# A windowed attention with a soft mixture of experts: the same steps in another hand-written order

## The chip, the cores and the metric

The program runs on one core of one Trainium2 chip. A core has five engines that run side by side, each through its own instructions in program order: TensorE (matrix products, PE in the profile; its loads of stationary operands are shown apart as PEld), VectorE (DVE), ScalarE (ACT), GpSimd (POOL) and SyncE (SP), which here issues nearly all DMA transfers. An instruction waits on semaphores until what it needs has been signalled; whatever stands behind it on the same engine waits with it. The metric is the device time of one execution in microseconds (us). Three runs of the kernel before took 214.01 to 214.91 us, the median is 214.57 us.

## The reference

The input is q, k and v of 4 batches, 8 heads, 768 positions and head width 64, and the weights of a soft mixture of 8 experts.

- Attention: scores q·k/8 plus a bias that falls with the distance (slope by head), over the 96 keys up to the position itself and 8 global keys; softmax over the keys; times v. The result, x, has 3072 tokens of width 512.
- Mixture: logits = x·phi (32 slots); softmax over the tokens gives the dispatch weights, and 32 slot inputs are weighted sums of tokens. Each expert runs its 4 slots through relu(s·w1)·w2 (512 to 1024 to 512). Softmax over the slots gives the weights with which each token mixes the 32 slot outputs.

```
scores = scale * q @ k.T + bias ; a = softmax(where(keep, scores, -1e9)) ; x = a @ v
logits = x @ phi ; d = softmax(logits, axis=0) ; slots = d.T @ x
out    = softmax(logits, axis=1) @ concat_e( relu(slots[e] @ w1[e]) @ w2[e] )
```

## The kernel before

**Units.** The attention is cut into 16 units u = 0 to 15 of one batch and two heads (a pair of heads, i = 0 and 1). The keys of a unit are cut into seven blocks of 120, each with the 8 global keys, and the queries that see a block are the 216 from its start. The steps of one unit, with their engine and the line that the profile gives for them:

- `load_qk(u)`, `load_v(u)` (SP, L389 and L392): the two transfers of the unit, into two buffers each (`raw`, `vt`) that take turns.
- `scores(u, k)`, k = 0, 1, 2 (PE, L521): products of keys and queries into one of two PSUM tiles `sc`, which also take turns.
- `biased(u, k)` (DVE, L530): adds the bias table, writes to `tb` and keeps a running maximum. The PSUM tile is free again behind it.
- `max_t(u)` (PE, L537) and `max_r(u)` (DVE, L542): maximum over the partitions.
- `exponential(u, i)` (ACT, L546), then `w_hi(u, i)` (ACT, L549; `w_hi_dve` on DVE, L552): the weights of head i, and their high part in 16 bits into `ph`.
- `w_lo(u, i, part)` (POOL, L556; `w_lo_dve` the same on DVE, also L556): the low part, in three pieces for each head.
- `v_hi(u)` (POOL, L489), `v_hi_act(u)` (ACT, L492) and `v_lo(u)` (DVE, L499): high and low part of V.
- `values(u, i)` (PE, L573): 39 products of the weights of head i with V into bank i of the one PSUM tile `x`; the text calls `values(u, 0)` the first product with V of a unit and `values(u, 1)` the second.
- `ev_sums(u)` (DVE, L586), `ev_recs(u)` (L592), `ev_mul(u, 0)` and `ev_mul(u, 1)` (L598): row sums, their reciprocals, and the scaling of X of each head out of `x` into `xn`; the scaling also keeps a maximum (`xmax`).
- `tr(u, k)` (PE, L610) and `tr_copy(u, k)` (ACT, L615; `tr_copy_dve` on DVE, L619): X transposed, in two parts.
- `logits` (PE, L640) every second unit; behind each batch the dispatch: `logits_all`, `strip_max`, `strip_exp`, `by_token` (PE, L696), `dispatch` (PE, L719), `dispatch_sum` (DVE, L730).

**The one tile `x`.** Both heads of a unit are written into one PSUM tile, and the waits that the compiled program gets go by that tile, not by its banks: a first product of unit u+1 waits for every scaling of unit u that stands ahead of it in the program, and a scaling of unit u that stands behind it waits for that product. (In the compiled program, `ev_mul(2, 1)`, which stands behind `values(3, 0)`, carries a wait for TensorE; where it stands ahead it carries none.)

```
565    x = xx[:, i]
573    nc.tensor.matmul(out=x[:, (D + 1) * t:(D + 1) * t + d], lhsT=w[:, c:c + P], rhs=vv[:, j, i, 0:d], ...
598    nc.vector.tensor_tensor_reduce(
599        out=xnb[(u // 2) % 3][:, :, c:c + D], in0=xv[:, i, :, 0:D], ...
819    for name, u, *args in ORDER:
820        steps[name](u, *args)
```

**What sets the order.** Nothing schedules at run time. `ORDER` (L51) is a list of 603 steps written out; the loop at L819 issues them in that order, and so each engine's program is the part of the list that falls to it.

**Weights.** w1 and w2 are 32 pieces of 1 MB each. Ten go into buffers of their own during the attention (`piece`, L372), some into holes of the attention's buffers (`extra`), and thirteen into those buffers when their last use is over (`free`). The rest follow when the first layer of the experts has used up its own buffers.

**The end.** Behind the last unit: the last dispatch (`last_dispatch`, L746), the first layer of the experts (`hidden`, PE, L106), transposes, the second layer (`project`, PE, L136), and the mixing of slot outputs with the output transfers (`combine`, PE, L196; copies L199 and L201).

Of the kernel before, what the change touches and what calls it, by code (L numbers as in the profile page):

```python
# [275 lines left out]
def tile_attention_moe(ctx: ExitStack, tc: tile.TileContext, qk, v, phi, w1, w2, nn, out):  # L276
# [64 lines left out]
    held = []  # L341
    for name, i, *_ in ORDER:
        if name == "free":
# [95 lines left out]
    def late_constants():  # L439
        nc.gpsimd.tensor_tensor(out=i4, in0=ident[:, 0:32], in1=ident[:, 32:64], op=ALU.add)  # L440
        nc.gpsimd.tensor_tensor(out=i4, in0=i4, in1=ident[:, 64:96], op=ALU.add)
        nc.gpsimd.tensor_tensor(out=i4, in0=i4, in1=ident[:, 96:128], op=ALU.add)
        nc.gpsimd.memset(sl, 0.0)
# [374 lines left out]
    late_constants()  # L818
    for name, u, *args in ORDER:  # L819
        steps[name](u, *args)  # L820
# [295 lines left out]
```

## Time and profile before

| | |
|---|---|
| median of three runs | 214.57 us (214.01 to 214.91) |
| the profiled execution | 215.71 us |
| its span, first to last instruction | 213.7 us |
| share of the span busy: PE, DVE, ACT, POOL | 84%, 69%, 59%, 45% |
| the 16 DMA engines | 61.38 MB, mean 287 GB/s |
| mean granted clock of TensorE | 0.971 of full speed |

The profiled execution took 1.14 us more than the median, and 2.0 us of it lie outside the span. The page of the profile gives the engines' busy time, the span in 40 slices, and the costliest groups of instructions. A view of waits adds up who stood idle for whom ("A <- B: us in total, times, longest"). A timeline lists instructions with their start, their duration and, in brackets, the idle time of the engine just before and what ended it. A table of windows gives the busy time of each engine in a stretch of time, with the granted clock and the DMA engines' share. The chain of waits is followed back from the last instruction.

### The profile page before, as it was taken

The numbers are of one execution on the slowest core, as the hardware profiler recorded it, in microseconds if no ns is written. First come the engines' busy times: TensorE is split into PE (matmuls) and PEld (weight loads), VectorE is DVE, ScalarE is ACT, GpSimd is POOL, SyncE is SP. The second block draws the span as 40 slices with busy tenths as digits, with TensorE's granted clock in tenths as the row PEclk, the third lists the DMA queues.
The fourth block names the chain that finished last, engine by engine and source line by source line (L and its number), as shares of the span: only waits on it lengthen the run. The fifth ranks groups of instructions, "written<-read, shape, count | busy, mean of one in ns | idle before, by whom it ended". The sixth has DMA issues, their size and how long they took to land.

```text
span 213.7 us, 6390 instructions
## 1 busy us (share of the span) xinstructions
PE 180.1 (84%) x2633; PEld 129.7 (61%) x2633; DVE 148.0 (69%) x382; ACT 125.9 (59%) x158; POOL 96.8 (45%) x122
## 2 busy tenths in 40 slices
PE   8999779699999899979897699588799999798400
PEld 2455679587878678667766588465353276475400
DVE  4869878479888597987977868877667745153600
ACT  2108768579998698897795879861303462041500
POOL 7113977567987688896584858430000000000000
PEclk9999999889999999999999999999999999999965
DMA  5946696748999999965538169959999999849892
GB/s 150 412 157 228 175 356 239 267 179 243 374 398 371 418 336 356 375 223 191 176 125 315 44 229 306 405 178 407 395 405 349 408 404 386 308 154 340 288 337 85
DMA packets 20630, 61.38 MB, mean 287 GB/s; under 512 B 1904, under 2 KB 9328, under 8 KB 18928
## 3 DMA queue, kind: packets, MB, share of 16 engines
q1 hardware_dynamic: 20448, 60.89, 77.4%
q8 instruction: 22, 0.36, 0.7%
q14 instruction: 16, 0.13, 0.2%
q10 hardware_dynamic: 144, 0.00, 0.0%
HBM read 54.59 MB, written 6.29 MB: 285 GB/s over the span
## 4 chain that ended last, share of the span: by engine, by line
PE 53%; DVE 17%; DMA 13%; ACT 7%; issue 4%; DVEq 0%; ACTq 0%; SPq 0%
PE sc L521 12%; PE x L573 12%; DMA raw<-in_qk_dram 8%; PE hp L106 6%; DVE tb L530 6%; DMA raw<-in_w_dram 5%; PE x L510 4%; PE x L136 3%; DVE xn L598 3%; ACT tb L546 3%; PE wp L424 2%; ACT ph L549 2%; PE m L640 2%; PE cp L196 2%; PE m L610 2%
## 5 line engine op out<-in xcount | busy, mean ns | idle before, releaser
L556 POOL TENSOR_TENSOR ph<-tb,ph 128x432 f16<-128x432 f32 x89 | 90.2, 1043 | 40.5 <-ACT ph L549 33.8
L573 PE MATMUL x<-v,ph 128*128 128x65 f16 (+1 forms) x1248 | 43.8, 194 | 10.2 <-DVE xmax L598 9.9
L573 PEld LDWEIGHTS <-ph 128*128 128x128 f16 x1248 | 41.7, 98 | 15.4 <-issue 14.2
L521 PE MATMUL sc<-raw 64*128 64x216 f32 (+2 forms) x448 | 48.3, 349 | 3.2 <-DVE mx L530 1.7
L546 ACT ACTIVATE tb<-tb,nb 128x1296 f32<-128x1296 f32 x32 | 44.0, 1375 | 9.3 <-DVE nb L542 9.3
L549 ACT CAST ph<-tb 128x1296 f16<-128x1296 f32 x31 | 39.4, 1271 | 15.5 <-PE x L573 13.5
L521 PEld LDWEIGHTS sc<-raw 64*128 64x128 f32 x448 | 38.2, 193 | 11.5 <-issue 4.8
L598 DVE CUSTOM_DVE_ANT_1 xn<-x,rc 120x448 f32<-120x448 f32 x32 | 19.6, 622 | 6.5 <-PE x L573 5.8
L530 DVE CUSTOM_DVE_ANT_1 tb<-sc,tt,mx 128x864 f32<-128x864 f32 x16 | 17.8, 1115 | 3.8 <-PE sc L521 3.4
L499 DVE SCALAR_TENSOR_TENSOR v<-vt,v 128x896 f16<-128x896 f32 x16 | 20.3, 1266 | 0.0
L492 ACT ACTIVATE v<-vt 128x896 f16<-128x896 f32 x14 | 13.2, 946 | 7.1 <-DMA vt<-in_v_dram 7.1
L610 PE MATMUL m<-ident,xn 120*128 120x120 f32 x105 | 16.4, 276 | 0.7 <-DVE al L657 0.4
L610 PEld LDWEIGHTS m<-ident,xn 120*128 120x128 f32 x105 | 10.8, 141 | 3.7 <-issue 1.6
L136 PE MATMUL x<-wp,vt 128*32 128x256 f32 x112 | 10.9, 381 | 1.1 <-DVE flag L856 1.1
L530 DVE CUSTOM_DVE_ANT_1 tb<-sc,tt 128x864 f32<-128x864 f32 x8 | 8.4, 1054 | 4.3 <-PE sc L521 4.0
L106 PE MATMUL hp<-wp,sl 128*32 128x512 f32 x80 | 10.5, 593 | 0.0
L530 DVE CUSTOM_DVE_ANT_1 tb<-sc,xta,mx 128x864 f32<-128x864 f32 x8 | 8.9, 1116 | 1.6 <-PE sc L521 1.3
L530 DVE CUSTOM_DVE_ANT_1 tb<-sc,xtt,mx 128x864 f32<-128x864 f32 x8 | 8.9, 1113 | 0.9 <-PE sc L521 0.6
L510 PE MATMUL x<-const-bfloat16-1.0 128*1 128x512 bf16 x37 | 8.7, 379 | 0.0
L199 ACT COPY tb<-cp 128x512 f32<-128x512 f32 x4 | 2.1, 590 | 10.9 <-PE cp L196 10.9
L199 ACT COPY ph<-cp 128x512 f32<-128x512 f32 x8 | 4.3, 604 | 6.4 <-PE cp L196 5.8
L136 PEld LDWEIGHTS x<-wp,vt 128*32 128x32 f32 x112 | 5.5, 110 | 3.8 <-DVE flag L856 1.2
(197 smaller groups left out, 261.0 us busy)
## 6 DMA issues: line engine op xcount, KB each, us to landing
raw<-in_qk_dram SPq DMA_DIRECT2D x15, 832.0 KB, 5.9
wp<-in_w_dram SPq DMA_DIRECT2D x10, 1024.0 KB, 8.5
vt<-in_v_dram SPq DMA_DIRECT2D x16, 448.0 KB, 5.8
wp<-in_w_dram SPq DMA_DIRECT2D x10, 512.0 KB, 7.5
out_dram<-ph SPq DMA_DIRECT2D x8, 512.0 KB, 6.9
tb<-in_w_dram SPq DMA_DIRECT2D x3, 1024.0 KB, 7.9
wp<-in_w_dram SPq DMA_DIRECT2D x8, 256.0 KB, 6.0
raw<-in_w_dram SPq DMA_DIRECT2D x8, 256.0 KB, 5.6
```

Source lines behind the costliest of these rows:

```text
L106: nc.tensor.matmul(out=hp[n][32 * s:32 * s + 32, :], lhsT=slv(a, c, s), rhs=w1(e, c // 2)[:, (c % 2) * DF + 512 * n:(c % 2) * DF + 512 * n ...
L136: nc.tensor.matmul(out=o[32 * s:32 * s + 32, 0:w], lhsT=ht[:, c, 32 * s:32 * s + 32], rhs=w2(4 * a + s, half)[:, c0 + c * w:c0 + c * w + w ...
L499: nc.vector.scalar_tensor_tensor(out=vlo[k].rearrange("p j i d -> p (j i) d"), in0=vraw[k].rearrange("p j i d -> p (j i) d"), scalar=V_SC, ...
L510: nc.tensor.matmul(out=xx[0:1, 0], lhsT=busy_in[:, 0:1], rhs=busy_in, start=True, stop=True)
L521: nc.tensor.matmul(out=z[:, i, at:at + n], lhsT=r_[r, KCOL[j]:KCOL[j] + KR], rhs=r_[r, KW + KB * j:KW + KB * j + n], start=True, stop=True)
L530: nc.vector.tensor_tensor_reduce(out=tb(u)[:, :, BW * k:BW * k + BW], in0=sc[(3 * u + k) % 2][:, :, 0:BW], in1=table.unit(u % NP, k), scal ...
L546: nc.scalar.activation(out=t, in_=t, func=AF.Exp, bias=nbs[u], scale=T_SC)
L549: nc.scalar.copy(out=blocks(phi_[i])[:, :, 0:QW], in_=tb(u)[:, i].rearrange("p (s c) -> p s c", c=QW))
L556: (engine or nc.gpsimd).tensor_tensor(out=blocks(plo_[i])[:, c, 0:QW], in0=tb(u)[:, i].rearrange("p (s c) -> p s c", c=QW)[:, c], in1=bloc ...
L573: nc.tensor.matmul(out=x[:, (D + 1) * t:(D + 1) * t + d], lhsT=w[:, c:c + P], rhs=vv[:, j, i, 0:d], start=(z == 0), stop=(z == len(ops) - ...
L598: nc.vector.tensor_tensor_reduce(out=xnb[(u // 2) % 3][:, :, c:c + D], in0=xv[:, i, :, 0:D], in1=rcs.pop((u, i)).unsqueeze(2).to_broadcast ...
L610: nc.tensor.transpose(out=m[:, at:at + KB], in_=xnb[(u // 2) % 3][:, t, P * (p % 2):P * (p % 2) + P], identity=ident[0:KB, 0:KB])
```

## The change

Only the list `ORDER` differs. It has the same 603 entries in number and the same work, issued in another order; the functions are untouched. Counted over the list:

- Low parts on VectorE (`w_lo_dve`): ten instead of seven (`w_lo` on GpSimd 86 instead of 89).
- Copies of the transposed X on VectorE (`tr_copy_dve`): six instead of eight (`tr_copy` on ScalarE 26 instead of 24).
- The one `w_hi_dve` (unit 15) becomes a `w_hi` on ScalarE.
- V's high part is made on GpSimd for units 11 and 15 instead of 0 and 8.
- Both scalings of a unit stand ahead of the next unit's first product for units 0 to 13. Before, the second one stood behind it for units 2, 5, 6, 12, 13 and 14; unit 14 is still so.
- The transfers: `load_v(1)` is the first one instead of the sixth; the ten pieces and most of the extras are spread differently among the loads of the units, the first piece later and the last ones later.

The list is one line of code in the file; here places of it are set apart in lines.

```diff
-ORDER = [('load_qk0', 0), ('load_phis', 0), ('load_qk', 0), ('keys', 0), ('scores', 0, 0),
+ORDER = [('load_v', 1), ('load_qk0', 0), ('load_phis', 0), ('load_qk', 0), ('keys', 0), ('table_even', 0),
...
-('ev_recs', 1), ('load_v', 3), ('max_r', 3), ('load_qk', 6), ('ev_mul', 1, 0), ('exponential', 3, 0),
-('v_hi_act', 3), ('biased', 4, 1), ('biased', 4, 2), ('ev_mul', 1, 1), ('values', 2, 0), ('scores', 5, 0),
+('ev_recs', 1), ('biased', 4, 1), ('ev_mul', 1, 1), ('load_qk', 5), ('tr', 0, 0), ('w_lo', 2, 0, 2),
+('ev_mul', 1, 0), ('piece', 2), ('scores', 5, 0), ('biased', 4, 2), ('w_lo', 2, 0, 1), ('w_lo', 2, 0, 0), ('values', 2, 0),
...
-('ev_recs', 11), ('scores', 14, 2), ('ev_mul', 11, 0), ('tr', 10, 0), ('logits_half', 9), ('biased', 14, 1), ('exponential', 13, 0),
-('v_hi_act', 13), ('biased', 14, 2), ('ev_mul', 11, 1), ('v_lo', 13), ('values', 12, 0),
+('ev_recs', 11), ('w_lo', 12, 0, 0), ('max_t', 13), ('load_qk', 15), ('ev_mul', 11, 1), ('max_r', 13), ('ev_mul', 11, 0),
+('biased', 14, 0), ('scores', 14, 1), ('logits', 9), ('w_lo', 12, 1, 2), ('biased', 14, 1), ('load_v', 14), ('values', 12, 0),
...
```

**TensorE, around the first product of unit 2.** `raw_93` and `raw_94` hold the q and k of even and odd units, `sc_167` and `sc_168` are the two score tiles, `ph_98` the weights of head 0, `ph_99` those of head 1. The loads of weights for L573 and most of its rows are left out. Before:

```order
L521 MATMUL sc_168<-raw_93 128x216 x4
L521 MATMUL sc_167<-raw_93 128x216 x2
L521 MATMUL sc_167<-raw_93 128x168 x2
L521 MATMUL sc_167<-raw_93 128x48 x2
L610 MATMUL m<-ident,xn_106 128x120 x4
...
L573 MATMUL x<-v_100,ph_98 128x65
...
L521 MATMUL sc_168<-raw_94 128x216 x4
L521 MATMUL sc_167<-raw_94 128x216 x4
L537 MATMUL m<-ident,mx 128x128
```

and with the change:

```order
L521 MATMUL sc_168<-raw_93 128x216 x4
L521 MATMUL sc_167<-raw_93 128x216 x2
L521 MATMUL sc_167<-raw_93 128x168 x2
L521 MATMUL sc_167<-raw_93 128x48 x2
L610 MATMUL m<-ident,xn_106 128x120 x4
L521 MATMUL sc_168<-raw_94 128x216 x4
...
L573 MATMUL x<-v_100,ph_98 128x65
...
L521 MATMUL sc_167<-raw_94 128x216 x4
L537 MATMUL m<-ident,mx 128x128
```

The first score step of unit 5 (`sc_168<-raw_94`) has moved ahead of the first product of unit 2.

**VectorE, the scalings of unit 11.** `tb_97` is the table buffer of unit 14, `xn_105` where the scaled X goes; a row with one output of one element reads out the running maximum of the row ahead. Before:

```order
L586 TENSOR_TENSOR rsall<-x,eps 120x14
L542 ISA m,nb<-m,shift 128x128
L542 ISA nb 128x1
L592 RECIPROCAL rc<-rsall 120x14
L598 ISA xn_105,xmax<-x,rc 120x7x64
L598 ISA xmax 120x1
L530 ISA tb_97,mx<-sc_168,xta,mx 128x2x432
L530 ISA mx 128x1
L530 ISA tb_97,mx<-sc_167,xta,mx 128x2x432
L530 ISA mx 128x1
L598 ISA xn_105,xmax<-x,rc 120x7x64
```

and with the change:

```order
L586 TENSOR_TENSOR rsall<-x,eps 120x14
L592 RECIPROCAL rc<-rsall 120x14
L598 ISA xn_105,xmax<-x,rc 120x7x64
L598 ISA xmax 120x1
L542 ISA m,nb<-m,shift 128x128
L542 ISA nb 128x1
L598 ISA xn_105,xmax<-x,rc 120x7x64
L598 ISA xmax 120x1
L530 ISA tb_97,mx<-sc_167,xta 128x2x432
L530 ISA mx 128x1
L530 ISA tb_97,mx<-sc_168,xta,mx 128x2x432
```

The two bias steps that stood between the scalings now come behind both; only the reduction of a maximum is between them.

**VectorE, between the scalings of unit 13 and the sums of unit 14.** `ph_99<-tb_97` are low parts of unit 14, `ph_98<-tb_95` and `ph_99<-tb_95` those of unit 15, L619 the copies, L552 the high part of unit 15, L499 V's low part. Before:

```order
L598 ISA xn_106,xmax<-x,rc 120x7x64
L598 ISA xmax 120x1
L556 TENSOR_TENSOR ph_99<-tb_97,ph_99 128x2x216
L619 COPY xta<-m 128x480
L619 COPY xta<-m 128x288
L556 TENSOR_TENSOR ph_99<-tb_97,ph_99 128x2x216
L552 CAST ph_98<-tb_95 128x6x216
L499 SCALAR_TENSOR_TENSOR v_100<-vt,v_100 128x896
L556 TENSOR_TENSOR ph_98<-tb_95,ph_98 128x2x216 x3
L586 TENSOR_TENSOR rsall<-x,eps 120x14
```

and with the change:

```order
L598 ISA xmax 120x1
L542 ISA m,nb<-m,shift 128x128
L542 ISA nb 128x1
L556 TENSOR_TENSOR ph_99<-tb_97,ph_99 128x2x216 x3
L499 SCALAR_TENSOR_TENSOR v_100<-vt,v_100 128x896
L730 SCALAR_TENSOR_TENSOR sacc<-sacc,al,m 128x512
L556 TENSOR_TENSOR ph_98<-tb_95,ph_98 128x2x216
L586 TENSOR_TENSOR rsall<-x,eps 120x14
```

The copies and the high part have left VectorE, one low part of unit 14 has come, two of unit 15 have moved behind, and the third dispatch sum has come ahead of the sums of unit 14.

2 lines of the change are left out of this document (1 added, 1 removed).

## The prediction

> **What bounds the kernel now.** I read the page's head first, then the table of windows, the waits, and the end of the timeline.
>
> ```profile
> span 213.7 us, 6390 instructions
> PE 180.1 (84%) x2633; PEld 129.7 (61%) x2633; DVE 148.0 (69%) x382; ACT 125.9 (59%) x158; POOL 96.8 (45%) x122
> ```
> ```profile
> 24.00:140.00 116.00, 101.60 (x1801) 85.44 (x1801) 94.12 (x241) 96.82 (x111) 84.70 (x84) 0.99 0.75 279
> 144.00:160.00 16.00, 13.76 (x177) 8.23 (x177) 10.86 (x42) 3.01 (x10) 0.00 (x0) 1.00 1.00 401
> ```
>
> The columns behind the stretch and its length are the busy time of PE, PEld, DVE, ACT and POOL, then granted clock, DMA share and GB/s. In 24 to 140 us, the units' steady part, TensorE is the busiest engine, 101.6 of 116 us. It stands 14.4 us there. No engine is full, so what ends its stands is what can be won.
>
> ```profile
> PE x L573 <- DVE xmax L598: 9.9, 10, 1.9
> DVE xn L598 <- PE x L573: 5.8, 4, 2.3
> PE sc L521 <- DMA raw<-in_qk_dram: 1.5, 3, 0.9
> ```
>
> Over the whole span TensorE stands 9.9 us, ten times, ahead of a first product with V until a scaling of the unit before is done (xmax is the scaling's read-out). VectorE stands 5.8 us ahead of a second scaling until the next unit's first product is done. Both come from the one tile x. Late loads of q and k cost TensorE 1.5 us.
>
> ```profile
> 158.16 7.49 PE L106 MATMUL hp<-wp,sl 128*32 128x512 f32 x66
> ...
> 186.04 1.50 PE L136 MATMUL x<-wp,vt 128*32 128x256 f32 x24 [1.12 <-DVE flag L856]
> ...
> 192.25 0.39 PE L136 MATMUL x<-raw,vt 128*32 128x256 f32 x2
> ```
> ```profile
> 181.78 4.15 DMA raw<-in_w_dram
> ```
>
> From 158.16 us on, TensorE runs through the experts with next to no stand; the one named is behind VectorE. The chain of waits names a weight transfer ahead of it, landing at 181.78 + 4.15 = 185.93 us; but the first product from that buffer is at 192.25, 6.3 us later. So the end is rigid behind the attention: if the attention ends earlier, the buffers are freed earlier and the transfers, full at share 1.00, move along; if they did not move at all, 6.3 us could still be won.
>
> **The change part by part: what it takes away.** Sums are against the profiled execution's 215.71 us.
>
> (a) Unit 1 to 2.
>
> ```profile
> 37.16 1.11 DVE L530 CUSTOM_DVE_ANT_1 tb<-sc,tt,mx 128x864 f32<-128x864 f32 x1
> ...
> 38.45 1.12 DVE L530 CUSTOM_DVE_ANT_1 tb<-sc,tt,mx 128x864 f32<-128x864 f32 x1 [0.18 <-PE m L610]
> ...
> 39.49 0.62 DVE L598 CUSTOM_DVE_ANT_1 xn<-x,rc 120x448 f32<-120x448 f32 x1
> ...
> 43.78 1.06 DVE L530 CUSTOM_DVE_ANT_1 tb<-sc,tt 128x864 f32<-128x864 f32 x1 [3.66 <-PE sc L521]
> ```
> ```profile
> 33.58 1.00 PE L521 MATMUL sc<-raw 64*128 64x216 f32 x8
> ...
> 40.17 1.71 PE L573 MATMUL x<-v,ph 128*128 128x65 f16 x39 [1.86 <-DVE xmax L598]
> ```
>
> The second scaling (39.49) waits behind the bias step of 38.45; TensorE stands 1.86 us until 40.17, and VectorE then 3.66 us for a score step queued behind that product. In the new order both scalings follow the bias step of 37.16, which ends at 38.27: done by 38.27 + 2 x 0.62 = 39.5. From 40.17 - 1.86 = 38.31 on TensorE has a score step to do, 1.00 us as at 33.58, up to 39.3. Of 1.86 us some 0.2 stay: **1.7 won**.
>
> (b, c, d) Units 8 to 9, 10 to 11 and 11 to 12.
>
> ```profile
> 94.25 1.12 DVE L530 CUSTOM_DVE_ANT_1 tb<-sc,xtt,mx 128x864 f32<-128x864 f32 x1
> ...
> 111.21 0.74 DVE L730 SCALAR_TENSOR_TENSOR sacc<-sacc,al,m 128x512 f32<-128x512 f32 x1
> 111.94 1.12 DVE L530 CUSTOM_DVE_ANT_1 tb<-sc,tt,mx 128x864 f32<-128x864 f32 x1
> ...
> 118.32 0.62 DVE L598 CUSTOM_DVE_ANT_1 xn<-x,rc 120x448 f32<-120x448 f32 x1
> ...
> 119.63 1.12 DVE L530 CUSTOM_DVE_ANT_1 tb<-sc,xta,mx 128x864 f32<-128x864 f32 x1 [0.68 <-PE sc L521]
> ...
> 121.94 0.62 DVE L598 CUSTOM_DVE_ANT_1 xn<-x,rc 120x448 f32<-120x448 f32 x1
> ```
> ```profile
> 95.97 1.33 PE L573 MATMUL x<-v,ph 128*128 128x65 f16 x39 [1.09 <-DVE xmax L598]
> ...
> 113.67 1.33 PE L573 MATMUL x<-v,ph 128*128 128x65 f16 x39 [1.89 <-DVE xmax L598]
> ...
> 122.62 1.33 PE L573 MATMUL x<-v,ph 128*128 128x65 f16 x39 [1.68 <-DVE xmax L598]
> ```
>
> b: the bias step between the scalings (1.12) goes behind them, more than the stand: **1.1**. c: the dispatch sum (0.74) and a bias step go: 1.12 + 0.74 = 1.86 of a stand of 1.89; **1.8**. d: from 118.32 + 0.62 to 121.94 VectorE does two bias steps and waits 0.68 for scores, 3.0 us, all gone from there; the whole stand: **1.7**.
>
> (e) The end.
>
> ```profile
> 137.08 1.02 DVE L619 COPY xta<-m 128x480 f32<-128x480 f32 x2
> 138.01 0.60 DVE L556 TENSOR_TENSOR ph<-tb,ph 128x432 f16<-128x432 f32 x1
> 138.53 0.83 DVE L552 CAST ph<-tb 128x1296 f16<-128x1296 f32 x1
> ...
> 140.28 1.64 DVE L556 TENSOR_TENSOR ph<-tb,ph 128x432 f16<-128x432 f32 x3
> ...
> 144.47 0.62 DVE L598 CUSTOM_DVE_ANT_1 xn<-x,rc 120x448 f32<-120x448 f32 x1 [1.42 <-PE x L573]
> ```
>
> VectorE runs here from scaling to scaling without a gap and is the chain. It loses two copies (1.02) and a high part (0.83) to ScalarE, and two of unit 15's three low parts (two thirds of 1.64, 1.1) to later; it gains a low part (0.60) and the dispatch sum (0.74): -1.02 - 0.83 - 1.1 + 0.6 + 0.74 = **1.6 won**. The 1.42 at 144.47 stays, since unit 14's second scaling still stands behind. ScalarE's load grows by the copies and a high part, some 2 us; it has 116 - 96.8 = 19 us spare in the steady part. Without that cover it would be 2 us.
>
> (f) The second scalings that stood behind a first product.
>
> ```profile
> 73.25 0.62 DVE L598 CUSTOM_DVE_ANT_1 xn<-x,rc 120x448 f32<-120x448 f32 x1 [2.34 <-PE x L573]
> ```
> ```profile
> 73.28 1.93 PE L719 MATMUL m<-xn,dn 120*32 120x256 f32 x28
> ```
>
> The words of the change are about these, yet while VectorE stood 2.34 us TensorE had its product, and the dispatch right behind. With 1.42 staying, the other three add up to 5.8 - 1.4 = 4.4: bounds 0 and 4.4; I take **0.5**, nearest the row that shows TensorE covered.
>
> (g) Loads. Pieces go from the crowded middle to later; the 1.5 us of stands for q and k: bounds 0 and 1.5, I take **0.7**.
>
> Gains: 1.7 + 1.1 + 1.8 + 1.7 + 1.6 + 0.5 + 0.7 = 9.1 us.
>
> **What it adds.** (h) First products of units 3, 6, 7, 13 and 14 now wait for a second scaling too: 0 to 5 x 0.62 = 3.1; mostly TensorE has other rows queued there; 1.0. (i) Bias steps and a dispatch sum moved behind scalings (four of 1.12 and 0.74 in a to d) hold back the score steps that wait for their tile: 0 to 5.2; each tile has a second one beside it, so I take 1.0. (j) Low parts on VectorE.
>
> ```profile
> 45.27 1.90 DVE L499 SCALAR_TENSOR_TENSOR v<-vt,v 128x896 f16<-128x896 f32 x1
> ...
> 122.49 1.08 DVE L499 SCALAR_TENSOR_TENSOR v<-vt,v 128x896 f16<-128x896 f32 x1
> ```
> ```profile
> 43.29 2.93 POOL L556 TENSOR_TENSOR ph<-tb,ph 128x432 f16<-128x432 f32 x3 [2.72 <-ACT ph L549]
> ```
>
> V's low part takes 1.08 us, and 1.90 where GpSimd is in its own low parts (43.29 to 46.22): 0.82 more. Some six of the ten low parts on VectorE (units 0, 7, 12, 15) now fall into such stretches, 0.6 to 1.4 each. Beyond the parts counted in e: 0 to 6 x 0.82 = 4.9; VectorE has 116 - 94 = 22 us spare in the steady part, so 0.5.
>
> The Trainium skill (SBUF — State Buffer, "SBUF: two separate sides") says that a VectorE instruction with two SBUF inputs and a GpSimd one exclude each other for the whole instruction; the trace agrees (1.90 against 1.08). It speaks against the change, and what it would do is priced in the first rival.
>
> (k) The load of V is issued first.
>
> ```profile
> 2.62 0.43 SPq L392 DMA_DIRECT2D vt<-in_v_dram x1
> ```
>
> It puts 0.43 us of issue and 448 KB (a VT tile of 128 x 896 x 4 bytes; at 401 GB/s 1.1 us) ahead of the first q and k: 0 to 1.5; the tables on VectorE cover most, 0.3. Costs: 1.0 + 1.0 + 0.5 + 0.3 = 2.8.
>
> **Sum:** 9.1 - 2.8 = 6.3; 215.71 - 6.3 = 209.4. The profiled execution lies 215.71 - 214.57 = 1.14 above the median. Taken over to unprofiled runs: 209.4 - 1.1 = **208.3 us**.
>
> ```profile
> 40.00:42.00 2.00, 1.82 (x41) 1.73 (x42) 0.12 (x2) 0.06 (x1) 0.57 (x1) 0.73 1.01 421
> 42.00:44.00 2.00, 2.00 (x12) 1.91 (x14) 0.22 (x1) 2.00 (x3) 0.71 (x1) 0.50 0.98 408
> ```
>
> Behind the stand of a the granted clock falls to 0.73 and 0.50, which costs 2 x 0.27 + 2 x 0.50 = 1.5 us here. I count nothing for it, as it may be just this execution's 1.14 above the median. The Trainium skill (TensorE: Matmul & The Clock Gate, "Part 1: The HAM clock gate") says the clock halves after an idle window of about 3.4 us; the trace differs, with half clock behind a stand of 1.86 us. By the rule the stand's removal changes nothing; by the row 1.5 us more are won, 206.8.
>
> **The rivals.** *Half of it comes back.* Steps pushed behind the scalings hold back scores, i at 5.2 instead of 1.0: gain 6.3 - 4.2 = 2.1, and 215.71 - 2.1 - 1.1 = 212.5 us. With j in full (4.9 instead of 0.5) in place of i it is 212.7: that is the mutual exclusion of VectorE and GpSimd on the path. For it: VectorE's work is the same and only moved, and it takes low parts on. Against: in c and d the scores that the moved bias steps hold back are not TensorE's next row, which is the first product; and VectorE has the 22 us spare.
>
> *No change.* The words hold for five more units only, f is nothing, and a to e return as stands in places that I cannot see: about 214.5. For it: only VectorE, not TensorE, stood in f. Against: a to d are stands of the busiest engine in the steady part.
>
> *Slower: TensorE stands at every unit.*
>
> ```profile
> 117.75 0.17 DVE L586 TENSOR_TENSOR rsall<-x,eps 120x14 f32<-120x14 f32 x1 [0.26 <-PE x L573]
> ```
>
> When a second product ends, VectorE does sums, a maximum and reciprocals (117.75 to 118.32, 0.57 us) and both scalings (2 x 0.62): 1.8 us, and where it is in a bias step at that moment, half a step more, 2.4. If TensorE has 1.3 us of rows (a score step and little more) ahead of the next first product, it stands 1.1 us at 15 units, 16.5 instead of 9.9; with only e and g won, 215.71 + 6.6 - 2.3 - 1.1 = 218.9. It decides from about 1.6 us of queued rows downward (15 stands of 0.8 make 12, the 9.9 of now and the 2.3). For it: in c TensorE had one score step there and stood. Against: the new order mostly has two score steps and a transpose or logits there.
>
> **How the numbers follow.** Forecast 0.56 (own range 205.5 to 211), half 0.25, no change 0.10, slower 0.09. Half a per cent, 1.07 us, is about what a measurement here can tell; faster than 213.5: 0.80, within: 0.11, slower: 0.09. The range reaches down to costs of nothing and f half in (9.1 + 2.0 us below 214.6, 203.5) and up to the half-returned gain with k in full, 212.5 + 1.2 = 213.7; what it leaves out is no change, slower, and a bit below.
>
> **What would show it.** The stands of TensorE for xmax fall from 9.9 us to under 5; those of VectorE for x from 5.8 to about 1.4; the experts' first row comes near 152 us instead of 158.16, with the rest of the span as long as before. I am wrong if stands of score steps for VectorE grow by what xmax loses, or if the experts stand for weights.

## The result: 204.74 us

The changed kernel took 204.74 us in the median of four runs (204.23 to 208.66), the kernel before 214.29 us beside it. The ratio is 0.9587, with an interval of 0.9466 to 0.9709: 6 to 11 us are won, 9 at the middle. 208.3 us was predicted. (Here and below a ratio leaves out the runs that lie more than 1.5% above the fastest of their kernel; a median takes in all.) The profiled execution took 204.23 us instead of 215.71, its span fell from 213.7 to 202.3 us.

The head of the page after, then its table of windows, with the columns as before (behind the stretch and its length the busy time of PE, PEld, DVE, ACT and POOL, then granted clock, DMA share, GB/s):

```profile
span 202.3 us, 6386 instructions
PE 177.6 (88%) x2633; PEld 128.0 (63%) x2633; DVE 146.5 (72%) x382; ACT 127.1 (63%) x161; POOL 93.5 (46%) x119
```
```profile
24.00:140.00 116.00, 110.22 (x1991) 91.65 (x1988) 102.58 (x265) 102.56 (x121) 86.82 (x86) 1.00 0.85 314
```
```profile
24.00:48.00 24.00, 21.39 (x365) 18.16 (x361) 21.78 (x54) 19.83 (x19) 18.82 (x20) 1.00 0.94 358
48.00:72.00 24.00, 24.00 (x442) 20.34 (x443) 21.01 (x59) 22.27 (x28) 19.77 (x21) 1.00 0.75 276
72.00:96.00 24.00, 24.00 (x443) 20.47 (x435) 21.99 (x57) 22.75 (x26) 20.03 (x21) 1.00 0.82 298
96.00:120.00 24.00, 24.00 (x439) 19.96 (x439) 22.91 (x58) 23.78 (x30) 19.14 (x20) 1.00 0.79 272
```

In 24 to 140 us TensorE is now busy 110.22 of 116 us, where it was 101.60; from 48 to 120 us it has no idle time left in any of the three rows. There it has become the bound.

The waits after (total, times, longest):

```profile
DVE tb L530 <- PE sc L521: 5.2, 5, 3.2
PE sc L521 <- DMA raw<-in_qk_dram: 4.4, 4, 1.5
PE x L573 <- DVE xmax L598: 2.2, 3, 0.9
```

The stands ahead of a first product fell from 9.9 us to 2.2. VectorE's stands ahead of a second scaling, 5.8 us before, have no row any more. TensorE's stands for q and k, however, went from 1.5 us to 4.4.

Two rows of TensorE's timeline, the first product of unit 2 and the start of the experts:

```profile
39.92 1.00 PE L521 MATMUL sc<-raw 64*128 64x216 f32 x8
40.94 1.33 PE L573 MATMUL x<-v,ph 128*128 128x65 f16 x39
...
146.84 7.49 PE L106 MATMUL hp<-wp,sl 128*32 128x512 f32 x66
```

The product with the stand of 1.86 us (a) now follows unit 5's score step without one. The experts start at 146.84 us instead of 158.16, 11.3 us earlier, and from there to the end it is 55.5 us as before: the tail moved along as a block, weights and all.

### The profile page after: what moved, and what is told of

It reads as the page before. It is cut to its first block, busy times and chain, and to the rows that moved or that the text cites. A ratio compares the mean times of both kernels' runs of the same rounds, so it can differ in the third digit from the quotient of the medians.

```text
span 202.3 us, 6386 instructions
## 1 busy us (share of the span) xinstructions
PE 177.6 (88%) x2633; PEld 128.0 (63%) x2633; DVE 146.5 (72%) x382; ACT 127.1 (63%) x161; POOL 93.5 (46%) x119
## 4 chain that ended last, share of the span: by engine, by line
## 5 line engine op out<-in xcount | busy, mean ns | idle before, releaser
L556 POOL TENSOR_TENSOR ph<-tb,ph 128x432 f16<-128x432 f32 x86 | 87.0, 1041 | 38.1 <-ACT ph L549 36.4
L521 PE MATMUL sc<-raw 64*128 64x216 f32 (+2 forms) x448 | 46.8, 341 | 4.4 <-DMA raw<-in_qk_dram 4.4
L573 PEld LDWEIGHTS <-ph 128*128 128x128 f16 x1248 | 41.2, 97 | 6.3 <-issue 6.0
L573 PE MATMUL x<-v,ph 128*128 128x65 f16 (+1 forms) x1248 | 43.1, 193 | 2.2 <-DVE xmax L598 2.2
L521 PEld LDWEIGHTS sc<-raw 64*128 64x128 f32 x448 | 36.8, 186 | 12.0 <-issue 3.4
L549 ACT CAST ph<-tb 128x1296 f16<-128x1296 f32 x32 | 40.7, 1271 | 4.8 <-PE x L573 4.1
L598 DVE CUSTOM_DVE_ANT_1 xn<-x,rc 120x448 f32<-120x448 f32 x32 | 18.9, 621 | 0.5
L499 DVE SCALAR_TENSOR_TENSOR v<-vt,v 128x896 f16<-128x896 f32 x16 | 18.2, 1135 | 0.2 <-ACT v L492 0.2
L510 PE MATMUL x<-const-bfloat16-1.0 128*1 128x512 bf16 x37 | 10.2, 422 | 0.0
```

What stands on the lines that cost most here:

```text
L499: nc.vector.scalar_tensor_tensor(out=vlo[k].rearrange("p j i d -> p (j i) d"), in0=vraw[k].rearrange("p j i d -> p (j i) d"), scalar=V_SC, ...
L521: nc.tensor.matmul(out=z[:, i, at:at + n], lhsT=r_[r, KCOL[j]:KCOL[j] + KR], rhs=r_[r, KW + KB * j:KW + KB * j + n], start=True, stop=True)
L549: nc.scalar.copy(out=blocks(phi_[i])[:, :, 0:QW], in_=tb(u)[:, i].rearrange("p (s c) -> p s c", c=QW))
L556: (engine or nc.gpsimd).tensor_tensor(out=blocks(plo_[i])[:, c, 0:QW], in0=tb(u)[:, i].rearrange("p (s c) -> p s c", c=QW)[:, c], in1=bloc ...
L598: nc.vector.tensor_tensor_reduce(out=xnb[(u // 2) % 3][:, :, c:c + D], in0=xv[:, i, :, 0:D], in1=rcs.pop((u, i)).unsqueeze(2).to_broadcast ...
```

## The experiments

Each is an edit of the list of steps. The runs of one kernel spread here by 0.4 to 3.3%, in part for a reason that the last section shows, so each median is read beside the profile of one of its runs. The experiments ran on three chips; the kernel before ran beside each group, and the ratios are against it.

**The changed kernel again.** Run on the same chip as three of the experiments below (f with a to d, the first loads, the loads ahead of pieces), as their control.

> The changed kernel itself once more, beside the next three on the same chip, so that they can be compared with it: 204.7 us as before, by every theory.

205.25 us (202.45 to 209.12), with the span of its profile at 202.4 us. The slower a run, the lower the mean granted clock: 0.977 at 202.45, 0.971 at 204.41, 0.960 at 206.08 and 0.940 at 209.12.

**Terms a to d alone.**

```diff
 # in the kernel before, units 1, 8, 10, 11
-ev_mul(u,0) ... bias steps, dispatch_sum ... ev_mul(u,1)  values(u+1,0)
+ev_mul(u,0)  ev_mul(u,1) ... bias steps, dispatch_sum ...  values(u+1,0)
-values(2,0)  scores(5,0)
+scores(5,0)  values(2,0)
```

> The kernel before, with the two scalings of units 1, 8, 10 and 11 side by side (the bias steps and the dispatch sum between them go behind), and the score step of unit 5 ahead of unit 2's first product: terms a to d of the prediction alone. The prediction's theory: 1.7 + 1.1 + 1.8 + 1.7 = 6.3 us won, less up to 1.0 for what is held back: 208 to 209. If the clock dip behind the stand of a goes too, 1.5 us more: 206.5. Rival, half of it comes back: the moved steps hold back scores, 6.3 - 5.2 = 1.1 us won (213.2).

206.54 us (204.91 to 207.37) beside 215.56; ratio 0.9651 [0.9550, 0.9752], about 7.5 us (5 to 10 by the interval). The waits of that run:

```profile
DVE xn L598 <- PE x L573: 5.2, 4, 2.3
DVE tb L530 <- PE sc L521: 3.7, 9, 0.7
PE x L573 <- DVE xmax L598: 2.2, 3, 1.1
```

TensorE's stands for the scaling fell to 2.2 us, as in the changed kernel, and score steps are not held back: VectorE's own waits for scores fell from 12.8 us to 3.7. Four places of one list gave most of the gain. What stays is VectorE's 5.2 us ahead of second scalings: 1.51 of it is unit 14's, the rest is f's.

**Unit 1 put back, in the changed kernel (a).**

```diff
 # in the changed kernel
-ev_mul(1,1) ... ev_mul(1,0) ... scores(5,0)  biased(4,2) ... values(2,0)
+ev_mul(1,1) ... biased(4,2)  ev_mul(1,0) ... values(2,0)  scores(5,0)
```

> The changed kernel, with unit 1 to 2 put back as it was: the second scaling of unit 1 behind two bias steps, unit 5's first score step behind unit 2's first product. The prediction's theory, term a: 1.7 us lost (206.2 from 204.5). If the granted clock falls again behind the stand, 1.5 us more, 207.7, and the clock row of that stretch shows it. Rival: the 1.05 us stand for q and k some 7 us later takes the delay up, so that only 0.6 us or less is lost (under 205.1).

206.79 us (205.47 to 209.90), 1.5 us above the control and 2.0 above the first runs. TensorE's stands from 30 to 50 us, with the table of windows behind the second:

```profile
35.34 1.00 PE L521 MATMUL sc<-raw 64*128 64x216 f32 x8 [1.41 <-DMA raw<-in_qk_dram]
43.56 1.33 PE L573 MATMUL x<-v,ph 128*128 128x65 f16 x39 [1.99 <-DVE xmax L598]
```
```profile
42.00:44.00 2.00, 0.44 (x15) 0.43 (x15) 1.51 (x4) 2.00 (x3) 2.00 (x3) 1.00 1.01 398
44.00:46.00 2.00, 2.00 (x42) 1.95 (x40) 0.02 (x1) 1.47 (x3) 0.88 (x1) 1.00 1.00 409
```

The stand is back, 1.99 us. Unit 6's stand for q and k, 1.05 us in the changed kernel, is gone in exchange: the load has that much more time. So a is worth less in this order than alone, about 0.9 us by these two stands. The medians say 1.5 to 2.0, but of the 2.4 us between the spans (204.7 and 202.3) 1.7 lie in the start, which the edit doesn't touch: unit 0's maximum (L537) comes at 19.56 us instead of 17.84. The clock stayed at 1.00 behind this stand.

**Units 8, 10 and 11 put back (b, c, d).**

```diff
 # in the changed kernel
-ev_mul(10,1)  ev_mul(10,0) ... values(11,0)  dispatch_sum(7) ... biased(13,2)
+ev_mul(10,1) ... dispatch_sum(7)  biased(13,2)  ev_mul(10,0)  values(11,0)
 # unit 11 with biased(14,0), biased(14,1) between, unit 8 with biased(11,1)
```

> The changed kernel, with units 8, 10 and 11 put back in kind: a bias step between the two scalings of unit 8, the dispatch sum and a bias step between those of unit 10, two bias steps between those of unit 11; the first product behind stays behind both. The prediction's theory, terms b, c and d: TensorE stands again ahead of three first products, 1.1 + 1.8 + 1.7 = 4.6 us lost (209.1 from 204.5). Rival: in the changed order TensorE has more rows queued there, so the stands come back in part only, under 2.3 us lost (below 206.8).

211.20 us (208.16 to 212.24); ratio to before 0.9802 [0.9628, 0.9976] where the changed kernel has 0.9587: 0.0215 of 214.3, 4.6 us, as the prediction's terms have it. The two intervals overlap, though, so it is the rows that show it. This profile is of one of the slower runs (211.43 us):

```profile
109.38 2.02 PE L573 MATMUL x<-v,ph 128*128 128x65 f16 x39 [1.81 <-DVE xmax L598]
118.30 1.33 PE L573 MATMUL x<-v,ph 128*128 128x65 f16 x39 [1.34 <-DVE xmax L598]
```
```profile
110.00:112.00 2.00, 2.00 (x30) 2.00 (x28) 0.88 (x2) 0.54 (x1) 0.00 (x0) 0.50 0.75 256
```

The stands are back with nearly their old sizes (1.81 against 1.89, 1.34 against 1.68, and unit 8's at 92.20 with 0.97 against 1.09), 4.1 us in all where the terms have 4.6, so the new order has few more rows queued there to cover them. Behind the first of the two the clock is at 0.50.

**Second scalings ahead, alone (f).**

```diff
 # in the kernel before, units 2, 5, 6, 12, 13
-ev_mul(u,0) ... values(u+1,0) ... ev_mul(u,1)
+ev_mul(u,0)  ev_mul(u,1) ... values(u+1,0)
```

> The kernel before, with one thing changed: the second scalings of units 2, 5, 6, 12 and 13 stand ahead of the next unit's first product with V, directly behind the first scaling. This is term f (and h) of the prediction alone. The prediction's theory: f wins 0.5 us and h costs about as much, since TensorE had its product while VectorE stood, so no change that can be told (214.3, within 1.1 us). Rival 1, f was undersized: VectorE's stands of 2.34 us and the like hold back bias steps and with them TensorE, so 2 to 4.4 us are won (210 to 212.3). Rival 2, TensorE now stands ahead of each of these first products: 5 x 0.6 to 1.1 us lost (217.3 to 219.8).

212.88 us (208.88 to 215.09) beside 215.56 (212.38 to 217.86): too much spread to tell by the medians. The profiles give an estimate. By the last section's count the one here has three falls of the clock and the one of before has one, 1.7 us each: 213.0 - 5.1 = 207.9 us of span against 213.7 - 1.7 = 212.0, about 4 us for f alone.

**f with a to d.**

> The kernel before, with terms a to d and f together: the scalings of units 1, 8, 10 and 11 side by side, the second scalings of units 2, 5, 6, 12 and 13 ahead of the next first product, unit 5's first score step earlier. Left out are the low parts and copies on VectorE, the order of the loads, and all else that is moved. Theory now: a to d alone gave 206.5; f adds 0.5 to 2; the rest of the change (e, g, j, k) sums to about nothing, so this is as fast as the changed kernel within 1 us: 204.5 to 206. Rival: the rest of the change wins too, and this stays 1.5 us or more behind the changed kernel.

203.88 us (203.29 to 204.04); ratio 0.9471 [0.9399, 0.9544], 11.3 us. That is 3.8 us more than a to d alone (0.9651 - 0.9471 = 0.018), on another chip and with intervals that nearly meet; by the spans of the profiles, 204.0 and 201.9, it is 2.1. In that profile of a to d TensorE stands 1.90 us at 127.37 for a copy on VectorE (L619), with a fall of the clock behind it that costs 1.7; with f the stand is 0.95 and the clock doesn't fall. This kernel is also a bit ahead of the changed one at 205.25: the rest of the change together wins nothing.

**f undone alone, on a quiet base.** With the loads' order mended (k, next) there is no clock dip in the profile and the runs lie close, so f was tried again there.

```diff
 # in the changed kernel with k's mend, units 2, 5, 6, 12, 13
-second scaling of u ... values(u+1,0)
+values(u+1,0)  second scaling of u
```

> The changed kernel with the loads in the old order (201.5 us), and the second scalings of units 2, 5, 6, 12 and 13 back behind the next unit's first product with V, as they stood before the change: the words of the change undone alone, in an order with no other stand to hide it. The prediction's theory: f is worth 0.5 us and h gives it back, since TensorE has its product meanwhile: 201 to 202, no change that can be told. Theory now: VectorE, 22 to 23 of 24 us busy in the stretches from 48 to 120 us, has no slack for five stands of up to a product's 1.35 us and more, and gives them on to TensorE: 2.5 to 4 us lost, 204 to 205.5, with stands of TensorE for VectorE (the scaling's read-out or score steps) that the changed kernel doesn't have in that stretch.

In units 2, 5 and 6 the second scaling of the changed order is that of head 0, which the next unit's first product writes over. So this kernel leaves out the scaled X of head 0 of these units and scales the next unit's instead; the instructions and their sizes are those of the old form. 205.57 us (204.65 to 208.46); ratio 0.9598 [0.9543, 0.9652] against 0.9359, so 4 us more than the base at 201.51 (5 by the ratios, as the two ran on two chips); the spans are 203.2 and 199.8 us. VectorE's timeline and TensorE's there:

```profile
46.15 0.63 DVE L598 CUSTOM_DVE_ANT_1 xn<-x,rc 120x448 f32<-120x448 f32 x1 [3.58 <-PE x L573]
46.70 0.08 DVE L598 DVE_READ_ACCUMULATOR2_ANT xmax<- 120x1 f32 x1
46.70 0.46 DVE L619 COPY xtt<-m 128x288 f32<-128x288 f32 x1
```
```profile
44.78 1.34 PE L573 MATMUL x<-v,ph 128*128 128x65 f16 x39
47.30 0.60 PE L610 MATMUL m<-ident,xn 120*128 120x120 f32 x4 [1.19 <-DVE xtt L619]
```
```profile
48.00:72.00 24.00, 22.62 (x402) 18.58 (x402) 20.55 (x56) 20.63 (x26) 18.13 (x19) 1.00 0.67 239
72.00:96.00 24.00, 22.68 (x421) 19.34 (x419) 22.62 (x57) 21.11 (x24) 18.88 (x19) 1.00 0.75 270
```

This is how f is paid. VectorE waits 3.58 us for the product that starts at 44.78; the scaling and a copy of transposed X stand behind on VectorE; and TensorE, done with the product, stands 1.19 us for that copy. The price isn't in the row of the wait: it goes to whatever stands behind it on VectorE, under another name. TensorE's busy time in 48 to 96 us falls from the base's 48.00 (24.00 twice) to 45.30.

**The order of the first loads (k).**

```diff
 # in the changed kernel
-load_v(1)  load_qk0(0)  load_phis(0)  load_qk(0) ... biased(0,0)  load_v(0)
+load_qk0(0)  load_phis(0)  load_qk(0) ... biased(0,0)  load_v(1)  load_v(0)
```

> The changed kernel, with the first load of V back behind the first q, k, positions and phi: it is issued sixth. Term k alone. The prediction's theory: k cost 0.3 us, so 0.3 won, which can hardly be told. Rival, from the changed kernel's trace: the start came 1.4 to 1.9 us later (the positions landed 1.5 us later, TensorE stood 1.17 and 0.65 us for q and k, and the granted clock fell behind it), so 1.4 to 1.9 us are won: 203. The first bias step then starts near 8.9 us instead of 10.05.

201.51 us (200.76 to 201.95), 3.7 us below the control, 2.6 by the spans (199.8 and 202.4); ratio 0.9359 [0.9286, 0.9431]. TensorE's start in the changed kernel, and then here (L510 are fillers):

```profile
7.22 1.00 PE L521 MATMUL sc<-raw 64*128 64x216 f32 x8 [1.17 <-DMA raw<-in_qk_dram]
8.87 1.29 PE L521 MATMUL sc<-raw 64*128 64x216 f32 x8 [0.65 <-DMA raw<-in_qk_dram]
10.09 4.77 PE L510 MATMUL x<-const-bfloat16-1.0 128*1 128x512 bf16 x15
...
17.84 0.32 PE L537 MATMUL m<-ident,mx 128*128 128x128 f32 x1
```
```profile
7.14 1.00 PE L521 MATMUL sc<-raw 64*128 64x216 f32 x8 [0.36 <-DMA raw<-in_qk_dram]
8.07 3.42 PE L510 MATMUL x<-const-bfloat16-1.0 128*1 128x512 bf16 x15
...
14.48 0.32 PE L537 MATMUL m<-ident,mx 128*128 128x128 f32 x1
```

Unit 0's maximum comes 3.36 us earlier: 1.17 + 0.65 - 0.36 = 1.46 us less of stands, and the fillers at full clock (3.42 us for 15 instead of 4.77) make most of it. In the control's profile, whose clock doesn't fall at the start, this row comes at 16.37 us, so 1.9 us are won without the clock. The start with V first is also uneven: in the five profiles that have it the row comes at 16.37 to 19.56 us, in the five without it at 14.48 to 14.60.

**Loads of q and k ahead of pieces (g).**

```diff
 # in the changed kernel
-load_v(2) ... piece(1) ... load_qk(4)      piece(2) ... piece(3) ... load_qk(6)
+load_qk(4)  load_v(2) ... piece(1)         load_qk(6)  piece(2) ... piece(3)
```

> The changed kernel, with two loads of q and k ahead of weight pieces: unit 4's ahead of V 2's and piece 1's, unit 6's ahead of pieces 2 and 3. Term g alone. The prediction counted 0.7 us won by late q and k loads; the changed kernel's trace shows the reverse, stands of 1.54 us at 33.75 and 1.05 us at 47.16. Theory now: both stands go, 2.0 to 2.6 us won: 202.4. Rival: the pieces, issued later, hold up the next loads instead, or TensorE stands for VectorE there, and under 0.7 us is won.

209.20 us (206.57 to 209.75), 4 us slower than the control. SP's queue, TensorE's stands and one of ScalarE's:

```profile
22.24 6.66 SPq L389 DMA_DIRECT2D raw<-in_qk_dram  x2
29.00 0.39 SPq L392 DMA_DIRECT2D vt<-in_v_dram  x1
29.44 0.42 SPq L372 DMA_DIRECT2D wp<-in_w_dram  x1
...
32.53 6.66 SPq L389 DMA_DIRECT2D raw<-in_qk_dram  x2
```
```profile
41.93 1.00 PE L521 MATMUL sc<-raw 64*128 64x216 f32 x8 [2.55 <-DMA raw<-in_qk_dram]
...
59.65 1.29 PE L573 MATMUL x<-v,ph 128*128 128x65 f16 x37 [1.97 <-POOL ph L556]
```
```profile
51.93 0.95 ACT L492 ACTIVATE v<-vt 128x896 f16<-128x896 f32 x1 [3.73 <-DMA vt<-in_v_dram]
```

A load of q and k can only be issued when its buffer is free. Each of the two long rows takes two loads together: unit 3's goes out at 22.24 us, unit 4's, put ahead, only at the row's end, 28.9, no earlier than the 28.2 us of the changed kernel. Meanwhile it holds SP's queue for some 6 us; V and the pieces behind it are issued in a lump at 29 us, and unit 5's load, issued at 32.53, lands behind them: a stand of 2.55 us where none was. A load of V comes late too: ScalarE stands 3.73 us for it ahead of V's high part, the exponentials and weights queued behind that on ScalarE come late, and so, by their order, do GpSimd's low parts, for which TensorE stands 1.97 us. The two stands that were to go did shrink (unit 4's to 0.40 us, unit 6's to nothing), but the next loads were held up, as the rival has it.

**Pieces apart, with k's mend.**

```diff
-piece(0) ... piece(1)     piece(2) ... piece(3) ... piece(4)
+piece(0)  piece(1)        piece(2) ... load_v(5)  piece(3) ... load_v(6)  piece(4)
```

> The changed kernel with the loads in the old order (201.5 us), and three weight pieces moved away from loads of q and k: piece 1 directly behind piece 0, where little is in transfer, piece 3 behind V 5's load and piece 4 behind V 6's. Theory: the stands for q and k of 1.77 us (unit 4) and 1.50 us (unit 6) are waits behind pieces of 1 MB, 2.6 us of transfer each; the second goes, the first falls to under 1, and 2 us or more are won: 199.5. Rival: as when the loads were put ahead of the pieces, which cost 4 us, the pieces only meet other loads: no gain or a loss of 1 to 3 us.

200.76 us (200.36 to 206.03); ratio 0.9357 [0.9312, 0.9403]. Unit 4's stand is gone, unit 6's is 1.19 us instead of 1.50, so it was unit 4's that piece 1 held up; what holds up unit 6's stays open. Beside 0.9359 the gain can't be told. With k's mend this is the fastest of all, 4 us ahead of the changed kernel.

**Low parts back on GpSimd (j).**

```diff
 # in the changed kernel with k's mend
-w_lo_dve(0,0,0) ... w_lo_dve(7,0,1) ... w_lo_dve(12,1,0)
+w_lo(0,0,0) ... w_lo(7,0,1) ... w_lo(12,1,0)
```

> The changed kernel with the loads in the old order (201.5 us), and three of the low parts that the change put on VectorE in the middle (of units 0, 7 and 12) back on GpSimd. Term j alone. The prediction's theory: they collide with GpSimd's own low parts and cost up to 0.82 us each, of which 0.25 us reaches TensorE: 201.3, no change that can be told; at most 2.5 us won (199.0). Rival: GpSimd, 85 of 116 us busy in the steady part, ends these low parts later than VectorE did and the products wait for them: 0.5 to 3 us lost.

203.93 us (203.54 to 206.47); ratio 0.9539 [0.9482, 0.9595] against 0.9359: 2.4 us lost by the medians, 2.1 by the spans (201.9 and 199.8). GpSimd and TensorE at unit 0:

```profile
21.50 3.90 POOL L556 TENSOR_TENSOR ph<-tb,ph 128x432 f16<-128x432 f32 x4 [1.31 <-ACT ph L549]
```
```profile
24.49 1.29 PE L573 MATMUL x<-v,ph 128*128 128x65 f16 x37 [1.73 <-POOL ph L556]
```

GpSimd takes 3.90 / 4 = 0.98 us for each low part, VectorE 0.60. With the fourth on GpSimd, unit 0's product stands 1.73 us for it; with it on VectorE the product has no such stand. A second stand for GpSimd, 0.82 us, comes at 113.56; near unit 7 there is none.

**The end's work back on VectorE (e).**

```diff
 # in the changed kernel with k's mend
-tr_copy(11,1), (12,0), (12,1)   w_hi(15,0)       w_lo(15,0,0), (15,0,1)
+tr_copy_dve, three times        w_hi_dve(15,0)   w_lo_dve, twice
```

> The changed kernel with the loads in the old order (201.5 us), and near the end what term e took off VectorE put back on it: the copies of units 11 and 12 (three), the high part of unit 15's first head and two of its low parts. Term e's own rows: 1.02 + 0.83 + 1.1 = 2.95 us more of work on VectorE between units 12 and 15, and TensorE ends that much later if VectorE is the chain there: 204.5. Rival: from 123 us on TensorE stood only 2.2 us for VectorE in the changed kernel, so VectorE has slack there, and under 1 us comes back: 201.5 to 202.5.

206.91 us (205.09 to 208.38), 5.4 us lost; ratio 0.9633 [0.9583, 0.9683]. TensorE's stands from 120 us on:

```profile
124.64 0.32 PE L537 MATMUL m<-ident,mx 128*128 128x128 f32 x1 [1.46 <-DVE mx L530]
126.57 1.33 PE L573 MATMUL x<-v,ph 128*128 128x65 f16 x39 [0.84 <-DVE xmax L598]
134.45 1.73 PE L573 MATMUL x<-v,ph 128*128 128x65 f16 x39 [2.95 <-DVE xmax L598]
```

They add up to 5.25 us. The base has 0.29, 0.72, 0.86 and 0.63 us there, 2.50: 2.75 us more, close to term e's 2.95 of rows. The rest isn't settled. The profile is of the slowest of the six runs, with a span 6.5 us above the base's: the clock falls behind the last of these stands (1.7 us), and unit 4's q and k stand 3.76 us instead of 1.77, which the edit doesn't touch, with a fall of the clock behind that too.

## Why the prediction was right, and where it wasn't

The direction, the place and, for a to e, the mechanism were right. The size was short by 3.6 us, with errors of both signs. 204.74 lies in the wide range, below the forecast's own 205.5 to 211; that it isn't further off is in part luck, as the errors of k and g offset part of those of f, i and j.

- **a to d, 6.3 us: right.** Alone they gave about 7.5 us, undone (b to d) 4.6 lost where the terms add up to 4.6 (4.1 by the stands). Only a is partly shared with the load of unit 6.
- **i, steps pushed behind, 1.0: too much.** VectorE's waits for scores fell, and no stand of scores grew. With that, and with j below, *half of it comes back*, which rested on i or j in full, falls.
- **f, 0.5: the step that failed most.** It measured 3.4 (spans) to 4 us undone, 2.1 (spans) to 3.8 with a to d. "Nearest the row that shows TensorE covered" was the false reading: TensorE was covered during VectorE's 2.34 us, but what stood behind on VectorE was late afterwards. The upper bound, 4.4, was close. The stands came under other names, as the copy's 1.19 us shows. The profile of before had such a stand to read, behind the second scaling of unit 13 that waited 0.55 us at 136.01 for its product:

```profile
137.88 0.41 PE L696 MATMUL m<-ident,ex 128*120 128x128 f32 x2 [1.90 <-DVE xta L619]
```

  It belongs to e's rows as well as to f: with f and without e it is 0.95 us.
- **h, 1.0: near.** In the changed kernel three stands for scalings are left, 2.2 us in all; of the five units of h one is among them, unit 14's first product with 0.72 us.
- **k, 0.3: undersized.** It cost 3.4 us by the start's rows, 1.7 of it by the clock, and 1.9 in the control's profile. The tables on VectorE didn't cover it: the positions, from which they are made, came late too. VectorE's first row on them starts at 4.33 us before, and after at:

```profile
5.81 0.17 DVE L797 CAST nf<-nraw 128x4 f32<-128x4 int32 x1 [2.91 <-DMA nraw<-in_n_dram]
```

- **g, 0.7 won: wrong sign.** The stands for q and k are 4.4 us instead of 1.5; 1.82 of it is k's; the rest, 2.6, is unit 4's load behind piece 1 and unit 6's, whose cause stays open.
- **j, 0.5 lost: wrong sign.** The collisions are there: two low parts on VectorE took 1.94 us together, 0.97 each instead of 0.60, while GpSimd was in its own.

```profile
131.29 1.94 DVE L556 TENSOR_TENSOR ph<-tb,ph 128x432 f16<-128x432 f32 x2 [0.20 <-ACT ph L549]
```

  But the three that were tried won 2.1 to 2.4 us on VectorE, since GpSimd was the one that TensorE waited for. The rule of the Trainium skill (SBUF — State Buffer, "SBUF: two separate sides") agrees with the longer rows; that it speaks against the change did not hold.
- **e, 1.6: its rows were right.** 2.95 us of work taken off showed as 2.75 us of stands when it was put back.
- **The clock, nothing: right by luck.** The profiles of before and after have one fall each, 1.7 us, and the same mean granted clock, 0.971: the fall behind a went, and one at the start came in its place. Without the one at the start, which is k's, 1.7 us more would have been won.
- *Slower: TensorE stands at every unit* falls: three stands for scalings, none over 0.9 us. *No change* falls too.

What was to show it: stands for xmax under 5 us (2.2), VectorE's for x near 1.4 (no row), the experts' first row near 152 us (146.84), the rest as long as before (55.5 us).

The terms don't add up strictly: 7.5 (a to d), 3.4 (f), 2.1 (j) and e's 1.6 as forecast, less 3.4 (k) and 1.1 (g, 2.6 of stands where 1.5 were), make 10.1, where the ratio says 9 and the profiled executions 11.5. They were measured in different orders, and one stand takes up another.

## What to carry to other kernels

When one engine waits in the middle of its queue, read what stands behind the wait on that engine, not only whether the engine it waits for is busy meanwhile: five scalings behind a product looked covered and cost 3.4 to 4 us. Before work is moved away from a slower engine or kept there, look at which of the two the bound engine waits for there: a longer row on the other one was cheap here. A load put ahead in a queue whose buffer isn't free yet only blocks what stands behind it.

## What the runs showed of the hardware

**The clock falls in fixed portions.** TensorE's granted clock, read in windows of 1 us from 3 to 150 us, stood near 1.00 or at 0.50. What the windows of one fall lack of 1.00 adds up to 1.70 or 1.71 us each time (before, from 40 us: 0.04 + 0.5 + 0.5 + 0.5 + 0.17), so each lasted 3.4 us and cost 1.7; once it was two in a row (8.5 to 15.3 us, with unit 1 put back, behind a stand of 2.13 us at the start):

```profile
8.00:12.00 4.00, 3.53 (x19) 1.94 (x18) 3.67 (x14) 0.95 (x1) 0.00 (x0) 0.56 0.67 278
12.00:16.00 4.00, 4.00 (x13) 1.24 (x12) 1.20 (x3) 0.00 (x0) 0.00 (x0) 0.59 0.00 0
```

All 15 falls in the profiles of this case begin within 1.5 us of the end of a stand of TensorE, or in it. Of the 21 single stands of 1.5 to 2.6 us, 11 were followed by one, and so were the two longer ones; shorter ones were not, but for pairs at the start (1.17 and 0.65 us in the changed kernel, 1.59 and 0.64 with q and k ahead of pieces; the pair of 1.33 and 0.65 in the control was not). The same stand, 1.89 us ahead of unit 11's first product, had a fall behind it with f alone and none in the profile of before. So a stand near 1.9 us costs, about every second time, 1.7 us more. The kernel before has five stands of 1.2 us or more from 24 to 140 us; the profiles with no stand over 1.3 us (f with a to d; pieces apart; f undone on the quiet base) show no fall, and f with a to d lay within 0.8 us in all its runs, where the kernel before spread over 2.7 beside it. Falls are not the whole of the spread: pieces apart had one run at 206.03 us, 5.3 above its median, with a mean clock of 0.963 against 0.973 in its profile, and what made it so slow stays open. That chance decides it fits the rule of the Trainium skill (TensorE: Matmul & The Clock Gate, "Part 1: The HAM clock gate") that a free-running window of about 3.4 us is watched; that a whole idle window is needed, as the page has it, the stands of 1.7 to 2.1 us contradict.
